# Decay tables in three transfers instead of eight, and two weight loads at other places in the load queue

## The chip, the cores and the metric

One NeuronCore of a Trainium2 chip runs the whole program. The metric is device time in microseconds (us), median of several executions. All transfers between HBM and the core's memory (SBUF) are issued from one queue, that of SyncE (SP), in program order. TensorE (PE) multiplies, VectorE (DVE), ScalarE (ACT) and GpSimd (POOL) do the elementwise work; each engine runs its instructions in program order and waits where an operand is not there yet.

## The reference

Three stages follow one another: an attention with decay, a gated product layer and a layer with a maximum of three products. In the attention (2 sequences, 8 heads, 768 positions, head size 64), a score between positions i and j of one chunk is multiplied by a power of the head's decay `lam`, and a state per head carries what lies before the chunk:

```python
Dmask = where(rel >= 0, lam ** rel, 0)            # rel = i - j inside a chunk
intra = ((q @ k.T) * Dmask) @ v
inter = (q * lam ** (i + 1)) @ kv_state
kv_state = lam ** block * kv_state + (k * lam ** (block - 1 - i)).T @ v
x = (x @ w_a) * (x @ w_b) @ w_out                  # 1536 tokens, 512 -> 1536 -> 512
x = max(x @ w1, x @ w2, x @ w3) @ w_out            # 512 -> 768 -> 512
```

The weights come as 64-bit numbers and are made fp32 on the chip; the products of the two layers run on TensorE with operands split in two (a high part in fp32r, and the rest).

## The kernel before, in words

The kernel uses chunks of C = 128 positions, so there are 12 attention units: `order` goes over 6 chunks and, within each, the 2 sequences. Unit n needs two loads of 512 KB each (`load`, L378): `aq{n}` (q and k, transposed) and `av{n}` (k and v). `scores(n)` (L389) makes 16 short matmuls from `aq{n}`; `masked(n)` (L415) multiplies them on DVE with the table `dmask`; `side(n)` (L401) makes two products with table values on POOL; `values(n)` (L424) makes the output and the new state on PE (L436, L441, L448), copies the output by ACT (L190) and updates the state by DVE (L460/L462) and ACT (L466).

The two tables are made once. `powers` (L334) computes the powers of all 8 heads on 8 partitions and writes them to HBM (`tab_d`, L346). From there they are read back as overlapping rows of 512 bytes: `tables` (L352) fills `dmask`, one row for each of 128 partitions and 8 heads, by four transfers of 128 KB; `decay_rows` (L357) fills `ltab`, by four transfers of 64 KB. In the order of heads that is wanted, odd heads are swapped between the two sides, and so each transfer covers every second column of one side.

The loop at L800 runs over the 12 units. In round n it queues the loads of `aq{n+4}` and `av{n+3}`, then makes `scores(n+2)`, `side(n+2)`, `masked(n+2)` and `values(n)` (round 0 makes `values(0)` first). From n = 7 on each round also makes one twelve-matmul piece of the first layer (`plain_group`, L545, line L555). So PE has a fixed order: scores, values, scores, values, and later a piece of the layer behind each.

Weights come in 33 items (`items`, L193). Item m is loaded by `load_to(m)` (L200), 1 MB in one transfer into one of two raw buffers `wr`, and turned into fp32 by the generator `converted` (L212): DVE L223, ACT L226, DVE L228, ACT L232, ACT L234, DVE L236; then `up_pair` (L241) splits it into a high part (ACT, L190) and the rest (DVE, L187). The class `Pace` (L57) decides at build time where on DVE, ACT and POOL these steps go between the attention's instructions: it keeps a model time for each engine, a rank for each task (lower goes first), and gates; a task whose gates are closed waits. `open_to("conv", m)` opens the conversion of item m, `open_to("split", m)` its split. The order that results is fixed in the program: if such a step has to wait for its weights, what stands behind it on DVE or ACT waits too.

Before the change, item 0 is loaded in round 2, behind `aq6` and `av5`, and opened in the same round; item 1 is loaded in round 7, behind `aq11` and `av10`, and opened there. Items 2 and 3 are loaded in round 9. Ranks (L304) are -1 for item 0, 0.5 for item 2, 1 for the others; the splits and sums of the attention's output have ranks 0 and 0.7.

Of the kernel before, what the change touches and what calls it, by code (L numbers as in the profile page):

```python
# [15 lines left out]
B, H, S, D = 2, 8, 768, 64  # L16
C = 128
NC = S // C
NP = H // 2
# [143 lines left out]
def decay_attention_gated_mlps(ctx: ExitStack, tc: tile.TileContext, qkv: bass.AP, lam: bass.AP, wup: bass.AP, wdown: bass.AP, out: bass.AP):  # L163
    nc = tc.nc
# [7 lines left out]
    pace = Pace()  # L172
# [27 lines left out]
    def load_to(n):  # L200
        while state["raw"] <= min(n, len(items) - 1):
            m = state["raw"]
            kind, i = items[m]
            t = wp.tile([128, 1024], I64, tag="r", bufs=2, name=f"wr{m}")
            if kind == "up":
                nc.sync.dma_start(out=t, in_=wup[i])
            else:
                nc.sync.dma_start(out=t[:, 0:WB], in_=wdown[i])
            raw[m] = t
            state["raw"] += 1  # L210
# [28 lines left out]
    wop, wtask = {}, {}  # L239
# [60 lines left out]
    def items_to(m):  # L300
        while state["item"] <= min(m, len(items) - 1):
            n = state["item"]
            kind, i = items[n]
            wtask[n] = pace.opens["done", n] = pace.add((up_pair if kind == "up" else down_block)(n, i), {0: -1, 2: 0.5}.get(n, 1))  # L304
            state["item"] += 1

    def open_to(what, m):
        if m < len(items):
            items_to(m)
            pace.open((what, m))  # L310

    def weights(i, name):
        m = at_item["up", i]
        items_to(m)
        pace.need(wtask[m], lambda: name in wop[m])
        return wop[m][name]

    def unit(first, k):
        b = first // 2 + k // 3
        m = at_item["down", first + (3 * (k // 3) * 512 // WB) + (0 if k % 3 == 0 else 1)]  # L320
        items_to(m)
        pace.need(wtask[m], lambda: (b, k % 3) in dunit)
        return dunit[b, k % 3]
# [6 lines left out]
    dmask = tables_sb[:, 0:1024].rearrange("p (g a i) -> p g a i", g=2, a=NP)  # L330
    ltab = tables_sb[:, 1024:1536].rearrange("p (a i) -> p a i", a=NP)
# [16 lines left out]
    def view(offset, ap):  # L348
        a = tab_d[:, :]
        return bass.AP(tensor=a.tensor, offset=a.offset + offset, ap=ap)  # L350

    def tables():  # L352
        for g in range(2):
            for odd in range(2):
                nc.sync.dma_start(out=dmask[:, g, odd:NP:2], in_=view((2 * odd + (g ^ odd)) * 2 * C, [[1, 128], [8 * C, NP // 2], [1, C]]))

    def decay_rows():  # L357
        for hh in range(2):
            for odd in range(2):
                nc.sync.dma_start(out=ltab[64 * hh:64 * hh + 64, odd:NP:2], in_=view((2 * odd + (hh ^ odd)) * 2 * C + C, [[0, 64], [8 * C, NP // 2], [1, C]]))  # L360


    order = [(b, c) for c in range(NC) for b in range(B)]
# [14 lines left out]
    def load(n, *which):  # L378

        if n >= len(order):  # L380
            return
        b, c = order[n]
        for i in which:
            of, name = ((aq, "aq"), (av, "av"))[i]
            of[n] = slot(f"{name}{n}")
            s = slice(512 if i == 1 and c == NC - 1 else 0, 1024)
            nc.sync.dma_start(out=of[n][:, s], in_=qkv[b * NC + c, i, :, s])

    def scores(n):  # L389
        if n >= len(order):  # L390
            return
        q, k = aq[n][:, 0:512], aq[n][:, 512:1024]
        banks = [bank(f"s{n}_{g}") for g in range(2)]
        for h in range(H):
            r, p = rows(h), h // 2
            o = slice(128 * p, 128 * p + 128)
            nc.tensor.matmul(banks[side_of(h)][:, o], k[r, o], q[r, o], start=True, stop=True)
        sc[n] = banks
        pace.pe(1.1)

    def side(n):  # L401

        if n >= len(order):
            return
        b, c = order[n]
        if c > 0:
            nc.gpsimd.tensor_tensor(out=aq[n][:, 1024:1536], in0=aq[n][:, 0:512], in1=ltab.rearrange("p a i -> p (a i)"), op=ALU.mult)
            pace.run("POOL", 512)
        if c < NC - 1:
            nc.gpsimd.tensor_tensor(  # L410
                out=av[n][:, 1024:1536].rearrange("p (h d) -> p h d", h=H), in0=av[n][:, 0:512].rearrange("p (h d) -> p h d", h=H),
                in1=dmask[:, :, :, C - 1:C].rearrange("p g a i -> p (g a) i").to_broadcast([128, H, D]), op=ALU.mult)
            pace.run("POOL", 400)

    def masked(n):  # L415
        if n >= len(order):
            return
        am[n] = slot(f"am{n}")
        for g in range(2):
            nc.vector.tensor_tensor(out=am[n][:, 512 * g:512 * g + 512], in0=sc[n][g], in1=dmask[:, g].rearrange("p a i -> p (a i)"), op=ALU.mult)  # L420
            pace.run("DVE", 512)
        sc.pop(n)
# [298 lines left out]
    with tc.manual_schedule():  # L721
# [15 lines left out]
        powers()  # L737
        load(0, 1)
        tables()
        load(2, 0)  # L740
        decay_rows()
        load(1, 1)
        load(3, 0)
# [56 lines left out]
        for n in range(len(order)):  # L800
            load(n + 4, 0)
            load(n + 3, 1)
            if n in (2, 7):
                m = n // 4
                load_to(m)
                open_to("conv", m)
                open_to("split", m)
            if n == 9:
                load_to(NPLAIN + 1)
                open_to("conv", NPLAIN)  # L810
            if n == 0:
                values(n)
            scores(n + 2)
            side(n + 2)
            masked(n + 2)
            if n > 0:
                values(n)
            if n % 6 == 5:
                j = n // 6
                xo[j] = Operands([xa[j, b] for b in range(B)], f"x{j}", Operands.PLAIN)  # L820
                for i in range(8):
                    pace.open((f"x{j}", i))
            if n == 10:
                pace.open(("x0", "sums"))
            if n > 6:
                next(layer1)
# [112 lines left out]
```

## Time and profile before

| what | us |
|---|---|
| median of 3 runs (lowest, highest) | 528.17 (527.85, 528.56) |
| the profiled execution, its own time | 528.49 |
| its span in the trace | 526.7 |
| PE busy | 508.4 (97% of the span) |
| DVE busy / ACT busy / POOL busy | 364.1 / 284.8 / 50.5 |
| mean granted TensorE clock | 0.99 of full speed |

The span is what the trace covers, the time of the execution lies 1.8 us above it. PE is busy for nearly all of the span: what it loses lies mainly in the first 50 us, where the attention runs and the loads come in. The 40 slices of the page show it: PE at 6 to 8 tenths in the first three, the granted clock at 7 tenths of full speed in the third, and the 16 DMA engines busy at 7 to 9 tenths in the first three.

### The profile page before, as it was taken

Reading aid. Unit: us, or ns where it says so; the run is one execution under the profiler, and the core shown is the slowest. Engines: PE = TensorE matmul, PEld = TensorE weight load, DVE = VectorE, ACT = ScalarE, POOL = GpSimd, SP = SyncE. Lnnn points to the kernel's source line nnn. Section 1 sums busy time; section 2 is a strip of 40 time slices with the busy share of each in tenths; the row PEclk is TensorE's granted clock in tenths of the full one; section 3 lists DMA queues with packets and bytes.
Section 4 is the critical chain, followed back from the end, with each engine's and each line's share of the span. In section 5 each row is a group of like instructions: output and inputs, shape, how many; then the busy total and the mean of one; then the engine's idle time right before and its main releaser. Section 6 shows DMA issues by size and latency. Waiting matters only on the chain.

```text
span 526.7 us, 7797 instructions
## 1 busy us (share of the span) xinstructions
PE 508.4 (97%) x3175; PEld 469.2 (89%) x3175; DVE 364.1 (69%) x546; ACT 284.8 (54%) x451; POOL 50.5 (10%) x46
## 2 busy tenths in 40 slices
PE   6879999999999999999999999998999999999997
PEld 3757899999999999998888888798999999988886
DVE  3267878886677766679969268385899998689000
ACT  1257754665545555367868366445476557366211
POOL 1673000011111111111000000000000000000000
PEclk9979999999999999999999999999999999999999
DMA  7995310222222111113542200100222211020221
GB/s 225 401 403 192 103 60 0 81 80 81 80 81 82 80 44 24 54 62 120 180 160 80 81 0 22 59 1 0 81 80 82 81 60 59 2 88 33 98 83 61
DMA packets 11812, 47.96 MB, mean 91 GB/s; under 512 B 1272, under 2 KB 3072, under 8 KB 9088
## 3 DMA queue, kind: packets, MB, share of 16 engines
q1 hardware_dynamic: 11776, 47.46, 25.1%
q8 instruction: 25, 0.41, 0.3%
q14 instruction: 11, 0.09, 0.1%
HBM read 44.30 MB, written 3.15 MB: 90 GB/s over the span
## 4 chain that ended last, share of the span: by engine, by line
PE 86%; DVE 5%; DMA 4%; ACT 2%; issue 1%; SPq 1%; ACTq 0%; DVEq 0%
PE yp L654 19%; PE zu L537 16%; PE zv L537 13%; PE out L700 9%; PE bu L537 8%; PE p L555 7%; PE bv L537 7%; PE xu L537 4%; PE xv L537 3%; DMA wr<-wup_dram 2%; DMA aq<-qkv_dram 1%; PE o L436 1%; DVE m L597 1%; ACT stt L466 1%; DVE lo L187 1%
## 5 line engine op out<-in xcount | busy, mean ns | idle before, releaser
L187 DVE TENSOR_TENSOR lo<-w,hi 128x1024 fp32r<-128x1024 f32 (+1 forms) x40 | 44.1, 1109 | 11.8 <-ACT hi L190 11.8
L190 ACT ACTIVATE hi<-w 128x1024 fp32r<-128x1024 f32 (+1 forms) x40 | 37.1, 952 | 12.8 <-DVE w L187 10.1
L654 PE MATMUL yp<-gh,dh 128*128 128x512 f32 x108 | 42.0, 389 | 0.0
L654 PE MATMUL yp<-gl,dh 128*128 128x512 f32 x108 | 42.0, 389 | 0.0
L654 PE MATMUL yp<-gh,dl 128*128 128x512 f32 x108 | 42.0, 389 | 0.0
L586 POOL TENSOR_TENSOR g<-z1u,z6u 128x384 f32<-128x384 f32 x20 | 25.1, 1258 | 172.8 <-DVE z6u L568 155.4
L236 DVE TENSOR_TENSOR w<-w,ws 128x1024 f32<-128x1024 f32 x21 | 26.5, 1262 | 16.0 <-ACT w L234 15.9
L187 DVE TENSOR_TENSOR gl<-g,gh 128x512 fp32r<-128x512 f32 x36 | 25.8, 725 | 13.3 <-ACT gh L190 13.3
L228 DVE SCALAR_TENSOR_TENSOR w<-wr,w 128x1024 int32<-128x1024 int32 (+1 forms) x26 | 31.0, 1193 | 0.2
L234 ACT ACTIVATE w<-w 128x1024 f32<-128x1024 f32 (+1 forms) x26 | 26.3, 1012 | 7.4 <-DVE w L228 7.2
L226 ACT ACTIVATE ws<-wr,bias 128x1024 f32<-128x1024 f32 x21 | 25.8, 1228 | 7.6 <-DMA wr<-wup_dram 7.6
L187 DVE TENSOR_TENSOR w<-w 128x256 f32<-128x256 f32 (+1 forms) x57 | 29.0, 509 | 0.8
L190 ACT ACTIVATE z7u<-zu 128x384 f32<-128x384 f32 x20 | 9.8, 491 | 35.5 <-PE zu L537 35.4
L689 DVE COPY ob<-out 128x256 f32<-128x256 f32 x1 | 0.4, 425 | 36.9 <-PE out L700 36.9
L654 PEld LDWEIGHTS yp<-gh,dl 128*128 128x128 f32 x108 | 20.3, 188 | 4.2
L654 PEld LDWEIGHTS yp<-gl,dh 128*128 128x128 f32 x108 | 20.3, 188 | 4.2
L232 ACT ACTIVATE ws<-ws,bias 128x1024 f32<-128x1024 f32 x21 | 24.0, 1144 | 0.0
L654 PEld LDWEIGHTS yp<-gh,dh 128*128 128x128 f32 x108 | 20.3, 188 | 4.1
L223 DVE TENSOR_SCALAR w<-wr 128x1024 int32<-128x1024 int32 (+1 forms) x26 | 17.5, 674 | 8.7 <-DMA wr<-wup_dram 8.6
L190 ACT ACTIVATE ob<-out 128x512 f32<-128x512 f32 (+1 forms) x12 | 7.0, 580 | 29.2 <-PE out L700 28.8
L568 DVE TENSOR_TENSOR z7u<-bu,z7u 128x384 f32<-128x384 f32 x20 | 11.1, 556 | 15.4 <-ACT z7u L190 15.4
L190 ACT ACTIVATE gh<-g 128x512 fp32r<-128x512 f32 x36 | 21.5, 618 | 0.0
(200 smaller groups left out, 1495.2 us busy)
## 6 DMA issues: line engine op xcount, KB each, us to landing
wr<-wup_dram SPq DMA_DIRECT2D x21, 1024.0 KB, 4.8
wr<-wdown_dram SPq DMA_DIRECT2D x12, 768.0 KB, 4.3
aq<-qkv_dram SPq DMA_DIRECT2D x12, 512.0 KB, 7.3
av<-qkv_dram SPq DMA_DIRECT2D x10, 512.0 KB, 9.6
out_dram<-ob SPq DMA_DIRECT2D x11, 256.0 KB, 2.0
tables<-tab_d SPq DMA_DIRECT2D x4, 128.0 KB, 3.7
av<-qkv_dram SPq DMA_DIRECT2D x2, 256.0 KB, 4.8
tables<-tab_d SPq DMA_DIRECT2D x4, 64.0 KB, 4.1
```

The source lines that it names most:

```text
L187: (nc.vector if e == "DVE" else nc.gpsimd).tensor_tensor(out=o, in0=a, in1=b, op=op)
L190: nc.scalar.activation(out=o, in_=a, func=AF.Copy)
L226: nc.scalar.activation(out=sign, in_=high.bitcast(F32), func=AF.Identity, bias=bias[:, 0:1])
L228: nc.vector.scalar_tensor_tensor(out=w, in0=low, scalar=29, in1=w, op0=ALU.logical_shift_right, op1=ALU.bitwise_or)
L232: nc.scalar.activation(out=sign, in_=sign, func=AF.Sign, bias=bias[:, 1:2])
L234: nc.scalar.activation(out=f, in_=f, func=AF.Abs)
L236: nc.vector.tensor_tensor(out=f, in0=f, in1=sign, op=ALU.mult)
L537: nc.tensor.matmul(ps, w, x, start=p in FIRST and i == 0, stop=i == len(todo) - 1, skip_group_check=p not in FIRST)
L555: nc.tensor.matmul(ps, w[:, 128 * k:128 * k + 128], x[:, k], start=m == 0, stop=m == 11)
L586: nc.gpsimd.tensor_tensor(out=ga[g.n][:, tokens(g.j, 0)], in0=g.z[1], in1=g.z[6], op=ALU.mult)
L654: nc.tensor.matmul(ps[e], w[:, cols], g, start=k == 0 and m == 0, stop=k == K1 - 1 and m == 2)
L700: nc.tensor.matmul(ps, a[:, o:o + 128], w[:, s], start=k == 0 and n == 0, stop=k == K2 - 1 and n == 2)
```

## The change

The eight table transfers become three: `dmask` is filled by one transfer of 512 KB, `ltab` by two of 128 KB, one for each half of the partitions. To make this possible, the host hands over `lam` in the order in which the table wants the heads. The bytes and the rows of 512 bytes are the same.

Item 0 is queued in round 0 (behind `aq4`, `av3`) instead of round 2 and opened in round 3 instead of 2. Item 1 is queued in round 3 (behind `aq7`, `av6`) instead of round 7 and opened in round 6 instead of 7. Item 3 gets rank 0.6 instead of 1.

```diff
-            wtask[n] = pace.opens["done", n] = pace.add((up_pair if kind == "up" else down_block)(n, i), {0: -1, 2: 0.5}.get(n, 1))
+            wtask[n] = pace.opens["done", n] = pace.add((up_pair if kind == "up" else down_block)(n, i), {0: -1, 2: 0.5, 3: 0.6}.get(n, 1))
...
     def tables():
-        for g in range(2):
-            for odd in range(2):
-                nc.sync.dma_start(out=dmask[:, g, odd:NP:2], in_=view((2 * odd + (g ^ odd)) * 2 * C, [[1, 128], [8 * C, NP // 2], [1, C]]))
+        nc.sync.dma_start(out=dmask.rearrange("p g a i -> p (g a) i"), in_=view(0, [[1, 128], [2 * C, H], [1, C]]))
 
     def decay_rows():
         for hh in range(2):
-            for odd in range(2):
-                nc.sync.dma_start(out=ltab[64 * hh:64 * hh + 64, odd:NP:2], in_=view((2 * odd + (hh ^ odd)) * 2 * C + C, [[0, 64], [8 * C, NP // 2], [1, C]]))
+            nc.sync.dma_start(out=ltab[64 * hh:64 * hh + 64], in_=view(hh * NP * 2 * C + C, [[0, 64], [2 * C, NP], [1, C]]))
...
-            if n in (2, 7):
-                m = n // 4
-                load_to(m)
-                open_to("conv", m)
-                open_to("split", m)
+            if n in (0, 3):
+                load_to(n // 3)
+            if n in (3, 6):
+                open_to("conv", n // 3 - 1)
+                open_to("split", n // 3 - 1)
...
-    arrays = {"qkv": qkv, "lam": np.asarray(inputs["lam"]).reshape(H, 1), "wup": wup, "wdown": wdown}
+    arrays = {"qkv": qkv, "lam": np.asarray(inputs["lam"])[[2 * a + (g ^ a % 2) for g in range(2) for a in range(NP)]].reshape(H, 1), "wup": wup, "wdown": wdown}
```

## Rows read from the trace of the kernel before

**Rows 1.** Chain of waits, in order of time: start us, length us, what.
```profile
48.15 2.51 PE p L555 x12
67.42 25.16 PE p L555 x144
```

**Rows 2.** Timeline of PE: start us, length us, engine, line, tiles, [idle before, releaser].
```profile
17.20 1.16 PE L397 MATMUL s<-aq 64*128 64x128 f32 x16 [0.86 <-DMA aq<-qkv_dram]
20.52 1.16 PE L397 MATMUL s<-aq 64*128 64x128 f32 x16 [0.66 <-DMA aq<-qkv_dram]
...
23.84 1.16 PE L397 MATMUL s<-aq 64*128 64x128 f32 x16
...
26.56 0.69 PE L448 MATMUL o<-av 128*64 128x64 f32 x16
30.74 2.33 PE L397 MATMUL s<-aq 64*128 64x128 f32 x16 [3.50 <-DVE am L420]
...
36.59 1.16 PE L397 MATMUL s<-aq 64*128 64x128 f32 x16
```

**Rows 3.** Timeline of DVE: the first and the last step of item 0.
```profile
29.39 0.70 DVE L223 TENSOR_SCALAR w<-wr 128x1024 int32<-128x1024 int32 x1 [8.64 <-DMA wr<-wup_dram]
...
40.31 1.85 DVE L187 TENSOR_TENSOR lo<-w,hi 128x1024 fp32r<-128x1024 f32 x1 [0.88 <-ACT hi L190]
```

**Rows 4.** Timeline of POOL, its waits for av3, av4, av5 and av6.
```profile
21.67 1.06 POOL L410 TENSOR_TENSOR av<-av,tables 128x512 f32<-128x512 f32 x1 [0.88 <-DMA av<-qkv_dram]
...
24.13 1.06 POOL L410 TENSOR_TENSOR av<-av,tables 128x512 f32<-128x512 f32 x1 [0.17 <-DMA av<-qkv_dram]
...
26.58 1.06 POOL L410 TENSOR_TENSOR av<-av,tables 128x512 f32<-128x512 f32 x1 [0.16 <-DMA av<-qkv_dram]
...
31.89 1.43 POOL L410 TENSOR_TENSOR av<-av,tables 128x512 f32<-128x512 f32 x1 [3.04 <-DMA av<-qkv_dram]
```

**Rows 5.** Windows: stretch, PE, PEld, DVE, ACT, POOL busy, clock, DMA share, GB/s.
```profile
6.00:7.00 1.00, 1.00 (x21) 1.00 (x20) 0.00 (x0) 0.00 (x0) 0.00 (x0) 1.00 0.83 299
7.00:8.00 1.00, 1.00 (x18) 0.76 (x15) 0.00 (x0) 0.00 (x0) 0.00 (x0) 1.00 0.77 250
8.00:9.00 1.00, 1.00 (x6) 0.49 (x5) 0.00 (x0) 0.00 (x0) 0.00 (x0) 1.00 0.83 142
...
10.00:11.00 1.00, 0.24 (x2) 0.19 (x2) 0.69 (x1) 0.00 (x0) 0.00 (x0) 1.00 0.98 286
11.00:12.00 1.00, 0.19 (x2) 0.00 (x0) 0.58 (x1) 0.00 (x0) 0.53 (x1) 1.00 1.01 384
12.00:13.00 1.00, 0.83 (x8) 0.83 (x10) 1.00 (x3) 0.00 (x0) 0.53 (x1) 0.54 1.33 242
...
29.00:30.00 1.00, 0.00 (x0) 0.00 (x0) 0.61 (x2) 0.55 (x1) 0.00 (x0) 0.57 1.02 418
```

**Rows 6.** Timeline of SP's queue: the table issues and the load behind them.
```profile
5.78 1.93 SPq L355 DMA_DIRECT2D tables<-tab_d  x4
...
8.26 2.62 SPq L360 DMA_DIRECT2D tables<-tab_d  x4
...
10.93 0.59 SPq L387 DMA_DIRECT2D av<-qkv_dram  x1
```

**Rows 7.** Timeline of DVE: the first products with the table.
```profile
10.02 0.69 DVE L420 TENSOR_TENSOR am<-s,tables 128x512 f32<-128x512 f32 x1 [5.59 <-DMA tables<-tab_d]
...
11.42 1.89 DVE L420 TENSOR_TENSOR am<-s,tables 128x512 f32<-128x512 f32 x3 [0.72 <-DMA tables<-tab_d]
```

**Rows 8.** The page's costliest groups: the third step of a conversion.
```profile
L228 DVE SCALAR_TENSOR_TENSOR w<-wr,w 128x1024 int32<-128x1024 int32 (+1 forms) x26 | 31.0, 1193 | 0.2
```

**Rows 9.** Windows as in rows 5, the stretch behind the first layer piece.
```profile
50.00:60.00 10.00, 10.00 (x147) 8.44 (x146) 9.39 (x15) 7.88 (x19) 0.00 (x0) 1.00 0.28 97
```

**Rows 10.** Waits of PE, whole span: waited for, us in total, times, longest.
```profile
PE bv L537 <- DVE lo L187: 1.7, 1, 1.7
```

**Rows 11.** Timeline of DVE: the first step of item 3.
```profile
94.90 0.69 DVE L223 TENSOR_SCALAR w<-wr 128x1024 int32<-128x1024 int32 x1
```

## The prediction

> **What bounds the kernel now.** I read the busy table and the slices first, then the chain of waits, then the timelines of the first 50 us, engine by engine. The slices show where PE is not full: only at the start. The chain shows the border: from 48.15 us, the first piece of the first layer, nearly every step is PE's own, and from 67.42 a run of 144 matmuls goes through without a gap [rows 1]. So the later stages are PE's arithmetic, and an edit before 48 us is worth what it moves that border, if the rest follows.
>
> Before the border PE's timeline has a rhythm, one round for each unit (scores, then values). The rounds begin at 17.20, 20.52, 23.84, then only at 30.74, then 36.59 [rows 2]. A clean round is the one from 23.84: it ends with the matmuls at 26.56 + 0.69 = 27.25, so 3.41 us. Then PE stands still for 30.74 - 27.25 = 3.49 us, and the row says for what: a mask product of DVE, whose result frees the score banks. DVE itself shows the reason: 8.64 us idle before the first step of item 0's conversion, waiting for the weights [rows 3]. The mask products stand behind that step. In the windows the granted clock falls to 0.57 at 29 to 30 us, after PE had stood since 27.25 [rows 5]; so the next round, from 30.74 to 36.59, takes 5.85 us, that is 5.85 - 3.41 = 2.44 us for the clock's lower level (1.2 instead of 2.4 GHz). One early step in DVE's order thus costs 3.49 + 2.44 = 5.93 us. The three rounds from 36.59 to 48.15 take 11.56 us, 1.33 more than three clean ones (10.23).
>
> What would stop PE next are the loads. POOL waits for av3 until 21.67, av4 until 24.13, av5 until 26.58, and for av6 until 31.89; DVE gets item 0 at 29.39 [rows 3, 4]. So the one queue delivers a pair of 512 KB loads in some 2.46 us and 1 MB of weights in 29.39 - 26.58 = 2.81 us, in the order of issue. PE waits 0.86 and 0.66 us for aq3 and aq4 [rows 2]: until about 24 us the delivery leads and PE follows.
>
> **The change, part by part.**
>
> *Opening item 0 a round later* takes its DVE step from ahead of one unit's mask products, and *its load two rounds earlier* brings the weights before aq5 instead of behind av5. Both together remove the wait: the weights land ahead of the load that PE needs for the round in which DVE gets to the step. Gain 5.93 us, if the clock stays up. The bounds: nothing, if the step is still late, and 5.93.
>
> The price is that aq5 comes later by one weight load, 2.81 us. Nothing shows aq5's landing; it lies between av3's (21.67) and av4's (24.13), taken as the middle, 22.9. Then it is 22.9 + 2.81 = 25.7, where PE would begin that round at 23.84 [rows 2, 4]: a new wait of 1.86 us. Bounds: 0.6 us (landing at 21.67) to 3.1 us (at 24.13). I take the middle, since the loads are of equal size. aq6 and av5 come 2.81 later as well, but PE's next round begins 3.41 after 25.7, and they are only 2.46 behind: hidden.
>
> *Item 1's load* goes past aq8 to aq11 and av7 to av10. aq8's old landing is about half a pair after av6, 31.89 + 1.23 = 33.1; with 2.81 more it is 35.9. PE gets to scores(8) three rounds after 25.7, at 35.9 to 36.9: a tie, cost 0, up to 0.4 if PE's rounds are clean and the loads aren't early. Item 1's buffer is a fresh one, so SP waits for nothing here, and the loads behind it that reuse slots wait for PE's values as before, only sooner.
>
> *The tables.* Behind them the delivery leads, so what counts is how full the DMA engines are. SP issues four transfers in 1.93 us and four in 2.62; one and two of them, at the mean of each group, are 0.48 and 1.31 us, and SP is at av1 some 2.8 us sooner [rows 6]. But the engines were at shares of 0.83, 0.77 and 0.83 from 6 to 9 us and full behind: 0.57 us is all the idle that earlier issues can fill [rows 5]. I take 0.4 us, between 0.57 and, if one transfer of 1024 rows runs worse than four, a loss (the fourth rival has its size).
>
> The page "DMA: Bandwidth & Descriptors" of the Trainium skill speaks against joining them: a transfer's semaphore is complete only when the data of all its engines have landed (section "Why a DMA increments its semaphore by 16 and not by 1"). The trace agrees in kind: the first half of the table released a mask product at 10.02, the second at 11.42 [rows 7]. By that rule the first product starts at about 11.4 - 0.4 = 11.0 us instead of 10.02; a row alone would allow 10.02. Either way the sum is the same, because PE reaches scores(3) early and waits 0.86 us for aq3 there [rows 2].
>
> *Item 1 opened a round earlier* puts DVE and ACT steps near the splits that the first layer piece needs. The splits have the lower rank and go first: cost 0. If two steps of it slip ahead, it is one L223 and one L228, 0.70 + 1.19 = 1.9 us [rows 3, 8]; this bound is a rival. Item 0 itself, from 29.39 to 40.31 + 1.85 = 42.16, takes 12.8 us [rows 3]; from 25.7 it would be ready at 38.5, ahead of the border.
>
> *Item 3's rank* moves its steps, from 94.90 on [rows 11], ahead of sums of the second half of x. PE's largest wait for a rest made by DVE in the whole span is 1.7 us [rows 10]; I take 0, between a loss of 1.7 and a gain of 1.7.
>
> *Smaller frictions.* The 1.33 us over three clean rounds come from DVE and ACT working off what had piled up behind item 0's wait. With no pile I take half away, 0.6 us (bounds 0 and 1.33).
>
> Sum: -5.93 + 1.86 - 0.4 - 0.6 = -5.07 us. The border moves from 48.15 to about 43.1. Made on the profiled execution, 528.49 becomes 523.4; that execution lies 0.3 above the median of 528.17, so the forecast is **523.1 us**.
>
> **The rivals.**
>
> *The clock falls at the new wait.* If the stand before aq5 takes TensorE to its lower level, a round is slow again: +2.44, so 525.5. For it: the fall at 12 to 13 us came after two microseconds in which PE was busy for 0.24 and 0.19 [rows 5], so less than the 3.49 us suffices. Also for it: 0.57 as the mean of one microsecond means that the clock was down from about 29.1 us, 1.9 us after PE stopped, and the new wait is as long. Against: the waits of 0.86 and 0.66 us brought no fall, and here PE works on right behind the wait. 28%.
>
> *Item 1 ahead of the splits:* +1.9, so 525.0. For it: one round less between opening and use. Against: rank. 10%.
>
> *Given back behind the border.* From 50 to 60 us DVE is busy for 9.39 of 10 us [rows 9]. If DVE sets the pace there, PE arrives early and waits, and at 67 us all but a fraction is gone: 0 to 1 us of gain, 527.2 to 528.2. Against: PE is busy for 10.00 of 10 in the same row, and item 0 leaves DVE earlier than PE arrives. 10%.
>
> *The joined transfers run worse (slower than before).* The tables' 768 KB are rows of 512 bytes, and the window from 8 to 9 us shows 142 GB/s at a share of 0.83 [rows 5]: 768 KB at that rate take 5.5 us. If joining halves the rate, everything behind comes 5.5 us later, up to aq5, because PE follows the delivery there; and the longer stand before the first mask product costs no more, as PE waits for the loads anyway. 5.5 + 0.4 more against the sum is +0.8, and a fall of the clock at the longer stand before scores(3), 2.44, makes +3.3: 531.4 us. It decides from a table time longer by about 85%, 5.07 - 0.4 = 4.67 of 5.5 us. Against: the same rows of the same bytes from the same queue. 7%.
>
> **How the numbers follow.** Forecast 45%, with a range of its own from 521.4 (friction gone, 0.7 us less, and a wait of 0.9 us) to 524.7 (aq5 as late as av4, 1.2 us more, and nothing from the tables, 0.4); the rivals 28, 10, 10 and 7%. About 0.2%, 1.06 us, is what a measurement of this kernel can tell from no change. The forecast and the first two rivals are faster by more, together 83%; the third splits around that bound and goes to "no change", 10%; the fourth is slower, 7%. The range is 520.9 to 527.2: it holds the forecast with its bounds, the first two rivals and the edge of the third, and leaves out somewhat less than 2 in 10.
>
> **What would show it.** Right, if in the changed kernel's timelines: DVE's first L223 stands after one more pair of mask products and has no idle time of several us before it; PE waits for aq5 once, by 1 to 3 us, at about 24 us; the granted clock stays at 1.00 from 24 to 45 us; the first row of L555 stands at about 43 us; from there to the end it takes as long as before. It is wrong if a wait of DVE for `wr` is still there, if a second low stretch of the clock follows, if L555 begins before 41.5 or after 45.5, or if the time from there to the end has grown by more than 1 us.

## The result, and the profile after

| kernel | median us | lowest, highest | executions | ratio to before, 95% interval |
|---|---|---|---|---|
| before | 528.27 | 527.39, 528.56 | 8 | |
| changed | 522.96 | 521.44, 526.12 | 8 | 0.9909 [0.9882, 0.9935] |
| forecast | 523.1 | range 520.9 to 527.2 | | |

The change made the kernel 5.3 us faster, close to the forecast. Its executions lie wider apart than those of before: two of eight took 526.0 and 526.1 us, with a mean granted clock of 0.99, and the lowest took 521.44, with 1.0. The profiled execution took 522.76 us with a span of 521.0, so its time is compared with the 528.49 us and 526.7 of before.

The page of the changed kernel, span, busy time and clock in 40 slices (compare the table and slices of before):

```profile
span 521.0 us, 7788 instructions
PE 506.4 (97%) x3175; PEld 467.7 (90%) x3175; DVE 365.4 (70%) x546; ACT 285.3 (55%) x451; POOL 51.5 (10%) x46
PEclk9899999999999999999999999999999999999999
```

Its PE timeline: the first products with the table (values(0)), then the beginnings of the rounds, from scores(3) on, and of the first layer piece (compare [rows 2]; columns as there):

```profile
12.10 0.43 PE L433 MATMUL o<-am,av 128*64 128x128 f32 x2 [1.55 <-DVE am L417]
...
16.95 1.70 PE L394 MATMUL s<-aq 64*128 64x128 f32 x16 [1.61 <-DMA aq<-qkv_dram]
...
21.12 1.16 PE L394 MATMUL s<-aq 64*128 64x128 f32 x16
...
24.47 1.16 PE L394 MATMUL s<-aq 64*128 64x128 f32 x16
...
27.80 1.16 PE L394 MATMUL s<-aq 64*128 64x128 f32 x16
...
37.95 1.16 PE L394 MATMUL s<-aq 64*128 64x128 f32 x16
...
41.28 0.62 PE L552 MATMUL p<-x0A,hi 128*128 128x384 f32 x2
...
43.54 0.44 PE L552 MATMUL p<-x0A,hi 128*128 128x384 f32 x1 [0.77 <-DVE x0A L187]
```

From 24.47 on the rounds are 3.3 to 3.5 us apart and run through to the first piece of the layer, which begins at 41.28 instead of 48.15 [rows 1]: 6.87 us earlier. The stand of 3.49 us on a mask product and the slow round behind it are gone. DVE's timeline says why: its first step of item 0 (compare [rows 3]; above it the first mask product, compare [rows 7]) has no idle time before it.

```profile
11.35 2.48 DVE L417 TENSOR_TENSOR am<-s,tables 128x512 f32<-128x512 f32 x4 [7.13 <-DMA tables<-tab_d]
...
25.33 0.68 DVE L223 TENSOR_SCALAR w<-wr 128x1024 int32<-128x1024 int32 x1
```

But there is no wait before the round at 24.47, that of scores(5), where I expected 1.86 us. And there is a low stretch of the clock that I did not place. Windows of the same trace show it (columns as in [rows 5]):

```profile
16.00:17.00 1.00, 0.06 (x2) 0.06 (x2) 0.68 (x2) 0.24 (x2) 1.00 (x2) 1.00 1.08 442
17.00:18.00 1.00, 1.00 (x12) 1.00 (x14) 0.00 (x0) 0.00 (x0) 1.00 (x1) 0.70 0.99 393
18.00:19.00 1.00, 1.00 (x11) 0.78 (x10) 0.30 (x1) 0.00 (x0) 0.83 (x2) 0.50 1.06 422
19.00:20.00 1.00, 1.00 (x14) 1.00 (x12) 0.99 (x2) 0.00 (x0) 1.00 (x2) 0.50 1.07 447
20.00:21.00 1.00, 1.00 (x22) 1.00 (x18) 0.00 (x0) 0.38 (x1) 0.73 (x2) 0.60 1.03 434
```

With the lower level at 0.50, these means put the clock low from about 17.4 to 20.8 us. PE had stood for 1.61 us before scores(3) and had been at work again since 16.95.

From the border to the end: the chain of waits gives the run of 144 matmuls 6 us earlier (61.43 against 67.42), so 0.9 us went back in between, 0.77 of it the wait for a split of x in the last PE row above.

```profile
61.43 25.16 PE p L552 x144
```

### The profile page after: what moved, and what is told of

Read it like the earlier page. It is cut to its first block, busy times and chain, and to the rows that moved or that the text cites. A ratio compares the mean times of both kernels' runs of the same rounds, so it can differ in the third digit from the quotient of the medians.

```text
span 521.0 us, 7788 instructions
## 1 busy us (share of the span) xinstructions
PE 506.4 (97%) x3175; PEld 467.7 (90%) x3175; DVE 365.4 (70%) x546; ACT 285.3 (55%) x451; POOL 51.5 (10%) x46
## 4 chain that ended last, share of the span: by engine, by line
PE 87%; DMA 6%; DVE 4%; ACT 1%; SPq 1%; issue 0%
PE yp L651 19%; PE zu L534 16%; PE zv L534 13%; PE out L697 9%; PE bu L534 8%; PE bv L534 7%; PE p L552 6%; PE xu L534 4%; DMA av<-qkv_dram 4%; PE xv L534 3%; DMA aq<-qkv_dram 2%; PE o L433 1%; DVE m L594 1%; PE o L438 0%; DVE lo L187 0%
## 5 line engine op out<-in xcount | busy, mean ns | idle before, releaser
L226 ACT ACTIVATE ws<-wr,bias 128x1024 f32<-128x1024 f32 x21 | 25.8, 1229 | 0.0
L417 DVE TENSOR_TENSOR am<-s,tables 128x512 f32<-128x512 f32 x24 | 15.3, 681 | 9.7 <-DMA tables<-tab_d 7.1
```

What stands on the lines that cost most here:

```text
L226: nc.scalar.activation(out=sign, in_=high.bitcast(F32), func=AF.Identity, bias=bias[:, 0:1])
```

## The experiments

They ran in three groups of four rows, each group beside the kernel before on a chip of its own; the kernel before took 528.8 us in each (medians 528.83, 528.88, 528.78). Runs of different groups are compared by their ratios.

| run | what it is | median us | ratio to before, 95% interval |
|---|---|---|---|
| tables_only | before, three table transfers | 528.48 | 0.9997 [0.9986, 1.0008] |
| loads_only | before, loads and openings | 526.55 | 0.9955 [0.9938, 0.9973] |
| no_rank | changed, item 3 at rank 1 | 526.72 | 0.9964 [0.9943, 0.9984] |
| warm_fill | changed, with matmuls of zeros | 522.95 | 0.9887 [0.987, 0.9903] |
| rank_only | before, item 3 at rank 0.6 | 529.77 | 1.0022 [1.0008, 1.0036] |
| load_early_open_old | changed, openings as before | 525.86 | 0.9943 [0.9927, 0.9959] |
| open_late_load_old | changed, loads as before | 524.82 | 0.9922 [0.9904, 0.994] |
| fill_load_next | warm_fill, loads in rounds 1 and 4 | 522.6 | 0.988 [0.9863, 0.9897] |
| after_again | the changed kernel once more | 521.67 | 0.9873 [0.9851, 0.9895] |
| fill_no_rank | warm_fill, item 3 at rank 1 | 526.61 | 0.9963 [0.995, 0.9975] |
| fill_old_tables | warm_fill, eight table transfers | 523.9 | 0.9908 [0.989, 0.9927] |
| fill_load_1_6 | warm_fill, loads in rounds 1 and 6 | 521.98 | 0.9874 [0.9859, 0.9889] |

**tables_only.** The new `tables` and `decay_rows` and the order of `lam`, nothing else.

> The kernel before with the three table transfers alone; loads, openings and ranks as before. Theory (the gain is DVE's wait for item 0 and the low clock behind it): both stay, DVE still idles 7 to 9 us before the first L223, so only the earlier delivery is left, 0.25 to 0.9 us as aq3 and av3 landed earlier in the changed kernel: 527.4 to 528.0 us beside 528.2. Rival (the tables carry the gain): 526 or less.

No difference that can be told: the tables alone bring a gain between -0.08% and 0.14%, which neither confirms nor rules out the 0.2 to 0.8 us of the theory. DVE still idles 8.21 us before item 0, and PE stands 2.93 us on a mask product and works at the low clock behind it:

```profile
30.11 2.35 PE L394 MATMUL s<-aq 64*128 64x128 f32 x16 [2.93 <-DVE am L417]
```

**loads_only and no_rank.** The first is the kernel before with the new loop block; the second the changed kernel with

```diff
-{0: -1, 2: 0.5, 3: 0.6}.get(n, 1)
+{0: -1, 2: 0.5}.get(n, 1)
```

> The changed kernel with the eight old table transfers and the old rank: the loads and the openings alone. Theory: no wait of DVE for the weights, first L552/L555 row at 41.5 to 43 us; the delivery is up to 0.9 us later, so PE stands 0.5 to 1.5 us before scores(5); 522.5 to 524.5 us. Rival (loads and openings need the tables' time): the stand before scores(5) is 2 us or more, the clock falls there, 525.5 us or more.

> The changed kernel with item 3 back at rank 1. Theory: PE waits nowhere between 61 and 189 us in either order, so no difference, 523.0 us like the changed kernel, and 61.43 to the end takes 459.5 us again. Rival (the rank brings or costs something): PE shows a wait of 0.5 us or more between 86 and 110 us, 523.5 us or more.

The theory failed for no_rank: most of the gain is lost, 0.36% is left. The border is where it should be (first L552 at 41.28 us in the chain). The time goes 58 us later, at the first products with item 3's weights, which the expectations call the third product group or pair (PE timeline; and DVE's first step of item 3):

```profile
99.49 0.61 PE L534 MATMUL zu<-x0A,hi 128*128 128x384 f32 x2 [1.52 <-ACT hi L190]
100.75 0.44 PE L534 MATMUL zu<-x0A,lo 128*128 128x384 f32 x1 [0.65 <-DVE lo L187]
```

```profile
90.16 0.69 DVE L223 TENSOR_SCALAR w<-wr 128x1024 int32<-128x1024 int32 x1
```

That is 2.17 us of waiting for item 3's split. In the kernel before, item 3 started at 94.90 [rows 11] and PE's first product with item 2 at 92.58; here PE is 7.1 us earlier (85.49), item 3 only 4.7. These are the chains of before and of no_rank:

```profile
92.58 1.04 PE zu L537 x6
```

```profile
85.49 1.04 PE zu L534 x6
```

The kernel before had little to spare there: its rest of item 3 was ready at 102.69 + 1.23 = 103.92, and PE took it at 105.25, 1.33 us later (DVE and PE of before):

```profile
102.69 1.23 DVE L187 TENSOR_TENSOR lo<-w,hi 128x1024 fp32r<-128x1024 f32 x1 [0.20 <-ACT hi L190]
```

```profile
105.25 0.33 PE L537 MATMUL zu<-x0A,lo 128*128 128x384 f32 x1
```

In the changed kernel, with rank 0.6, item 3 starts at 82.99, and PE goes through:

```profile
82.99 0.69 DVE L223 TENSOR_SCALAR w<-wr 128x1024 int32<-128x1024 int32 x1
```

In the windows of this profile the wait costs more than itself, because the clock falls too; first no_rank, then the changed kernel in the same stretch:

```profile
95.33:105.33 10.00, 7.83 (x35) 7.20 (x34) 7.46 (x12) 5.81 (x8) 1.06 (x1) 0.83 0.17 53
```

```profile
95.33:105.33 10.00, 10.00 (x60) 10.00 (x59) 8.64 (x12) 6.38 (x9) 1.02 (x1) 1.00 0.11 36
```

loads_only, which has the old rank too, has the same stand of 2.17 us at 100.66, without the fall. Its median lies about as much, 2.05 us, above what was expected at most, while its border behaved as expected (42.4 us in the chain, a stand of 1.49 us for aq5, before scores(5)):

```profile
25.71 1.16 PE L397 MATMUL s<-aq 64*128 64x128 f32 x16 [1.49 <-DMA aq<-qkv_dram]
```

loads_only and no_rank differ by the table transfers alone, and they ran on one chip: 526.55 us with eight transfers, 526.72 with three. So beside the moved loads, too, this pair shows no gain of the tables. no_rank's profile has the wait before scores(5) as well, 1.88 us; the row names a step of ACT as the releaser, but the start, 1.15 us ahead of av4 on POOL, fits aq5's landing as in loads_only (1.16 us).

**warm_fill.** Matmuls of zeros where PE stands, into a bank that is overwritten afterwards: six ahead of scores(3), and 14 instead of 8 ahead of values(0):

```diff
+        for i in range(fill):
+            nc.tensor.matmul(banks[0], warm[:, 0:128], warm, start=True, stop=True)
...
-        keep_warm(8)
+        keep_warm(14)
...
-            scores(n + 2)
+            scores(n + 2, {1: 6}.get(n, 0))
```

> The changed kernel with six idle-time matmuls of zeros ahead of scores(3), into a bank that scores(3) then overwrites, and 14 instead of 8 ahead of values(0). Theory (the spread of 521.4 to 526.1 us is a fall of the clock at the stands before values(0) and scores(3)): clock 1.00 from 5 to 45 us, every execution at 521.2 to 522.2 us. Rival (PE follows the delivery anyway, and waits for aq5 instead): a wait of 0.5 us or more before scores(5), and 522.5 us or more; or the fall moves there and the spread stays.

The theory is half right. The clock held (1.00 in the profile, 0.999 and 1.0 in all six executions) and the highest execution was 524.26 us, where the changed kernel had 526.12. But the executions still lie from 521.65 up, so the clock is not the whole spread. The median did not move either, as the rival said; PE waits for aq5 and for aq8, before scores(5) and scores(8):

```profile
25.29 1.16 PE L396 MATMUL s<-aq 64*128 64x128 f32 x16 [1.45 <-DMA aq<-qkv_dram]
36.46 1.16 PE L396 MATMUL s<-aq 64*128 64x128 f32 x16 [1.11 <-DMA aq<-qkv_dram]
```

**rank_only.** The kernel before with `3: 0.6`.

> The kernel before with item 3 at rank 0.6 and nothing else. Theory (the rank only guards the place at the third product group, where the kernel before has about 1 us to spare and the changed one without the rank stands 2.2 us): no difference, within 0.15% of before, PE without a wait from 67 to 195 us. Rival (the order with the rank is better anywhere): faster by 2 us or more.

Neither: it is 0.2% slower. In its profile PE loses 0.64 us in ten, waiting for a step of ACT (z6u) and not for item 3, where the kernel before loses none (10.00). The rest of the 0.2% (1.1 us) is not placed:

```profile
102.55:112.55 10.00, 9.36 (x55) 9.04 (x54) 8.32 (x14) 6.90 (x10) 1.57 (x2) 1.00 0.29 105
```

**load_early_open_old and open_late_load_old.** Half of the move each, with the three table transfers and rank 0.6 of the changed kernel. The loop block of each, put on fewer lines:

```python
            if n in (0, 3): load_to(n // 3)          # load_early_open_old
            if n in (2, 7): open_to("conv", n // 4); open_to("split", n // 4)
...
            if n in (2, 7): load_to(n // 4)          # open_late_load_old
            if n in (3, 7): open_to("conv", n // 4); open_to("split", n // 4)
```

> The changed kernel with the conversions opened where they were before (rounds 2 and 7). Theory A (the load's place alone removes the wait): item 0 lands at about 23.2 us, DVE stands 1 us or less before its first L223, PE does not wait for a mask product; like the changed kernel, 521.5 to 524.5 us. Theory B (the later opening is needed): a stand of 2 us or more of PE before scores(6) or scores(5) on a mask product, 525.5 us or more.

> The changed kernel with the loads where they were before (rounds 2 and 7) and item 0 opened in round 3, item 1 in 7. Theory A (the early load is needed): DVE waits for item 0 until about 28.5 us with the next unit's mask products behind it, PE stands before scores(7) until about 31 us, 1 us or less as PE needs until 30.5 for what is free, so most of the gain is there too: 522.5 to 525 us; PE does not wait for aq5. Theory B (the later opening is worth nothing without the load): a stand of 2.5 us or more and the clock falls, 526.5 us or more.

Each half alone brings 0.6 to 0.8%, where the whole change brought 0.9% in one group of runs and 1.3% in another. With the early load and the old opening DVE still idles 3.32 us (DVE below), more than the 1 us expected, but PE stands on no mask product before scores(5) or scores(6). The median, 525.86 us, is that of theory B without its stand. What is lost in this profile lies elsewhere: a low clock from 13 to 17 us, behind a stand of 2.29 us before values(0); a stand of 1.34 us before scores(5) (the row names ACT's step L226 of item 0; the start, 1.15 us ahead of av4, would fit aq5's landing too); and waits of 0.80 and 0.83 us at the first layer pieces. With the late opening and the old load DVE's idle time is 5.75 us instead of 8.64 [rows 3]; PE's stand moves one round on, to scores(7), and the clock falls there. PE and DVE of the first, then DVE and PE of the second:

```profile
25.37 1.16 PE L394 MATMUL s<-aq 64*128 64x128 f32 x16 [1.34 <-ACT ws L226]
```

```profile
24.03 0.69 DVE L223 TENSOR_SCALAR w<-wr 128x1024 int32<-128x1024 int32 x1 [3.32 <-DMA wr<-wup_dram]
```

```profile
29.87 0.69 DVE L223 TENSOR_SCALAR w<-wr 128x1024 int32<-128x1024 int32 x1 [5.75 <-DMA wr<-wup_dram]
```

```profile
32.48 2.67 PE L394 MATMUL s<-aq 64*128 64x128 f32 x16 [2.60 <-DVE am L417]
```

So the stand of 2.6 us with a fall of the clock, theory B's sign, was there in this profile, at 526.07 us the slowest of six; the median, 524.82 us, is what theory A gave.

**fill_load_next and fill_load_1_6.** warm_fill with item 0 in round 1 and item 1 in round 4 or 6:

```diff
-            if n in (0, 3):
-                load_to(n // 3)
+            if n in (1, 4):          # fill_load_1_6: (1, 6) and n // 6
+                load_to(n // 4)
```

> The kernel with the matmuls of zeros and, besides, item 0 queued one round later (round 1, behind aq5 and av4) and item 1 in round 4 (behind aq8 and av7). Theory (what is left is the wait for aq5, 1.45 us, and for aq8, 1.11 us, each behind a weight load): both waits gone, DVE stands 0.5 us or less before its first L223, 520.3 to 521.8 us. Rival (the delivery is full, and a wait moves behind the next load): waits of 1 us or more before scores(6) or scores(9), or of DVE for item 0, 522.5 us or more.

> The kernel with the matmuls of zeros, item 0 queued in round 1 and item 1 in round 6, behind aq10 and av9, where its conversion is opened. Theory (each 1 MB load costs PE what the next loads come later; item 1 is not needed before 47 us): no wait before scores(9), item 1 still lands before 47 us, 520.3 to 522.0 us, at most the 522.6 us of item 1 in round 4. Rival (what is left is not item 1's load): the same waits of 0.5 to 1 us a round earlier or later, 522.4 us or more.

The wait for aq5 is gone in both. In fill_load_next others stand in its place, before scores(6), (7) and (9) (PE below), and DVE idles 1.62 us before its first L223, where 0.5 or less was expected; 522.6 us is the rival's time:

```profile
26.72 1.16 PE L396 MATMUL s<-aq 64*128 64x128 f32 x16 [0.53 <-ACT ws L226]
30.52 1.16 PE L396 MATMUL s<-aq 64*128 64x128 f32 x16 [0.40 <-DMA aq<-qkv_dram]
37.99 1.16 PE L396 MATMUL s<-aq 64*128 64x128 f32 x16 [0.74 <-DMA aq<-qkv_dram]
```

With item 1 in round 6 the last of these is gone, but 0.40 and 0.82 us appear at the first layer pieces, and 0.63 us before scores(6) stays; 521.98 us lies at the upper edge of its theory. Neither ratio is clear of the changed kernel's 0.9873 in after_again (intervals overlap). But their executions lie close together: 521.7 to 523.2 us over nine.

**after_again, fill_no_rank and fill_old_tables.**

> The changed kernel once more, beside the next three on the same chip. Theory: 0.989 to 0.993 of the kernel before; executions in two groups by the clock, near 521.5 to 523.5 us without a fall beyond 3 us of low clock, near 526 us with one.

> The kernel with the matmuls of zeros (six ahead of scores(3), 14 ahead of values(0)), with item 3 back at rank 1. Theory (without the rank PE stands 2.2 us at the first products of the third pair, plus 0 to 2 us when the clock falls there): 2.2 to 4.3 us above the 522.95 us of the kernel with the matmuls of zeros and rank 0.6: 525 to 527.3 us. Rival (the difference seen without the rank came from the clock in the first 25 us): 523.5 us or less, no wait at 95 to 105 us.

> The kernel with the matmuls of zeros and rank 0.6, with the eight old table transfers. Theory (the joined transfers bring 0.5 to 1.2 us at the load that PE waits for, aq5, once item 0's load stands ahead of it): scores(5) 0.5 to 1.2 us later than the 25.29 us of the kernel with three transfers, 523.4 to 524.2 us. Rival (they bring nothing, as with the loads at their old places): 522.9 us or less.

after_again came out lower than expected, at 0.9873 of before instead of 0.989 to 0.993. It had one execution of six at 525.12 us (mean clock 0.993), the others from 521.25 to 522.37. Its profile is one without a fall of the clock, and there stands the wait that I had forecast, before scores(5). Even so the first layer piece begins at 40.85 us:

```profile
16.29 1.16 PE L394 MATMUL s<-aq 64*128 64x128 f32 x16 [1.49 <-DMA aq<-qkv_dram]
...
19.33 1.16 PE L394 MATMUL s<-aq 64*128 64x128 f32 x16 [0.39 <-DMA aq<-qkv_dram]
...
24.21 1.16 PE L394 MATMUL s<-aq 64*128 64x128 f32 x16 [1.49 <-DMA aq<-qkv_dram]
...
40.85 0.62 PE L552 MATMUL p<-x0A,hi 128*128 128x384 f32 x2
```

fill_no_rank confirms the rank with the early clock held: from the run of 144 matmuls to the last layer takes 411.2 us (chain: 61.45 to 472.63) where after_again takes 407.0 (59.96 to 467.00), so 4.1 us. Of these 2.17 are the stand, and the clock of 0.66 behind it accounts for about 1.7 of the rest (0.34 of 5 us). Two of its twelve executions had a mean clock of 1.0 and still took 525.85 and 526.04 us; no trace of these was kept, so what they lost beside the stand is open.

```profile
100.00:105.00 5.00, 3.74 (x12) 3.43 (x13) 4.55 (x6) 2.85 (x4) 0.00 (x0) 0.66 0.00 0
```

fill_old_tables is 0.2% above warm_fill, scores(5) at 25.81 instead of 25.29 us. The intervals of the two overlap, and three of its six executions had a lower clock (0.997, 0.997, 0.993) in spite of the matmuls of zeros, so not all of the 0.2% need be delivery. With the medians of loads_only and no_rank equal, the tables' share beside the moved loads stays open, between nothing and about 1 us.

## Why the prediction was right, point by point

- *The wait removed, 5.93 us:* right in place, and in size as far as the border shows it. No profile of a kernel with both the early load and the later opening shows the stand before scores(6) on a mask product. I had told the two edits as one, but each half alone brings a part, 3.0 and 4.1 us of the 5.3 to 7.1 us of the whole.
- *The new wait for aq5, 1.86 us:* the place was right, the size a little off: 1.49 us in after_again, loads_only and fill_no_rank, 1.45 in warm_fill. In no_rank it was 1.88. A part of the difference is the 2.81 us for 1 MB. In after_again POOL's waits for av3 and av4, with the weights and aq5 between them, end at 20.48 and 25.37 (POOL below): 4.89 us for 2 MB, where [rows 4] show 2.46 for a pair of 1 MB, so the weights cost 2.43. In the first profile of the changed kernel there is no wait, because the low clock from 17.4 to 20.8 us brought PE there later: scores(5) starts at 24.47 there and at 24.21 in after_again, where PE waited.

```profile
20.48 1.06 POOL L407 TENSOR_TENSOR av<-av,tables 128x512 f32<-128x512 f32 x1 [0.65 <-DMA av<-qkv_dram]
...
25.37 1.06 POOL L407 TENSOR_TENSOR av<-av,tables 128x512 f32<-128x512 f32 x1 [2.61 <-DMA av<-qkv_dram]
```

- *The tables, 0.4 us:* alone nothing that can be told from zero; beside the moved loads open, as said above. The first mask product starts at 11.35 and 10.82 us in the two profiles of the changed kernel, against the 11.0 that I had worked out. In all ten profiles with three transfers it starts between 10.5 and 12.2 us, in the four with eight between 9.7 and 10.2, with a second wait behind it. This agrees with the rule that a transfer's semaphore is complete only when all of its data have landed (the page "DMA: Bandwidth & Descriptors" of the Trainium skill, "Why a DMA increments its semaphore by 16 and not by 1"). In the two profiles of the changed kernel scores(3) then still waits for aq3, 1.61 and 1.49 us.
- *Frictions, 0.6 us:* all 1.33 went: the last three rounds take 41.28 - 31.13 = 10.15 us instead of 11.56. The border moved by 6.87 us, and by 7.30 in after_again, and not by 5.07. The missing wait is not the reason, since after_again has it. scores(5) starts at 24.47 and 24.21 us, where the sum has 25.7 - 0.4 = 25.3, and the five rounds behind it take 16.8 and 16.6 us, where the sum has 17.8. Of the 6.87 us 0.9 went back behind the border and 0.3 in the last stretch, so the span lost 5.7.
- *Item 1 a round earlier, 0:* 0.77 us of waiting for a split of x at the first layer piece in one profile, none in the other. Item 1's first step comes behind that piece in both (47.56 and 46.76 us), so the wait is not its doing.
- *Item 3's rank, 0 with bounds of 1.7:* this step failed. I looked at PE's waits in the kernel before and wrote 0; I did not ask whether that place would still have time to spare once PE came 7 us earlier. In the changed kernel the rank saves a stand of 2.17 us, and 4.1 us in the profile in which the clock falls behind the stand. That the forecast held all the same is luck: the rank is part of the change and kept PE from waiting, which is what 0 had assumed; without it the gain would have been 0.4%. In the kernel before the same rank costs 0.2%.
- *The rivals:* the clock fell in some executions, as the first rival said, but in the first profile behind the stand of 1.61 us before scores(3), and in after_again's profile not at all, not even at aq5. Three of the 14 executions of the changed kernel took 525.1 to 526.1 us, with mean clocks of 0.99 or 0.993; no trace of these was kept, so where their clock fell is not shown. "Given back behind the border" is what no_rank shows, though 58 us behind it and through the order of item 3's steps. The joined transfers did not run worse.
- *The prediction's own signs:* DVE's first step without a wait came as said, and so did the clock of 1.00 from 24 to 45 us; the wait for aq5 came in one of the two profiles. Two signs of being wrong came too. The first layer piece begins at 41.28 and 40.85 us, before 41.5; and the first profile takes 479.7 us from there to the end, 1.2 us more than the 478.5 of the kernel before, where 1 us was the limit (after_again: 478.7). So the number is closer than its parts, and that is in part luck: a border that came 1.8 us earlier than in the sum was paid back in part behind it, and in some executions by the clock. In the group of after_again the gain was 7.1 us.

## What to carry to other kernels

A step put early into an in-order queue costs what stands behind it: move its load ahead or the step back. Here each alone helped, and both together more. When a stage moves forward, look at the next places with little to spare: the kernel before had 1.3 us at item 3's first products, and most of a gain made 50 us earlier would have gone there. An edit that brings nothing in the old kernel (here it cost 0.2%) may be what keeps the gain in the new one, so it is tested with the rest of the change, not alone.

## What the runs showed of the hardware

The granted clock fell behind some stands of PE and not behind others of the same length, with the same program. In the first profile of the changed kernel a stand of 1.55 us before values(0) brought no fall (1.00 from 12 to 17 us), and one of 1.61 us before scores(3) did (low from about 17.4 to 20.8). In after_again stands of 1.52, 1.49 and again 1.49 us brought none. The 14 executions of this kernel take 521.3 to 526.1 us, and the three slowest have mean clocks of 0.99 or 0.993.

Six matmuls of zeros in one stand and six more in another went with a mean clock of 0.999 or 1.0 in all 15 executions of the three kernels that have them with rank 0.6 and three table transfers, none above 524.3 us; without them 4 of 14 had such a clock. It is no sure remedy: with eight table transfers three of six executions fell below (0.997, 0.997, 0.993, up to 525.6 us). And warm_fill's six still lie between 521.7 and 524.3 us at a full clock; the cause of that spread is open.
